# Attention with two expert layers: other weight slots lent to the first eight units, fewer conversions through borrowed slots, single-chunk stores

## The chip, the cores and the metric

The kernel runs on one core of one Trainium2 chip. The metric is the device time of one execution in microseconds (us). Before the change the median of three runs is 1017.11 us (1017.07 to 1017.4). Engines are named as in the profile: PE is the matrix engine, DVE the vector engine, ACT the activation engine, POOL the GpSimd, SP the engine that issues every DMA here.

## The reference

The inputs are q, k, v of shape (4 batches, 8 heads, 576 positions, 64) in float32. Three stages follow each other:

```
q_d, k_d, v_d = means over groups of 4 positions        # 144 positions
out_d  = softmax(q_d k_d^T / 8) v_d, repeated 4 times   # coarse attention
out_l  = softmax over |i - j| < 4 of q k^T / 8, times v # local attention
x  = out_d + out_l                                      # 2304 tokens x 512
y1 = (silu(x Wg) * (x Wv)) Wo                           # 512 -> 1536 -> 512
out = prelu(y1 Win, alpha) Wout                         # 512 -> 2048 -> 512
```

The softmax is written out with its maximum and sum; everything is float32 at the interface.

## The kernel before, in words

**Precision.** A float32 product is made of three passes of a rounded format: each operand is split into a high part and a low part, and hi*hi, hi*lo and lo*hi are summed in PSUM (`mm3`, L472 to L475). The weights arrive as 8-byte elements and are first turned into float32 by bit operations, then split (`w_split`, L124 to L143).

**Weights and slots.** The first layer has 12 slices j of 128 hidden columns, and for each a tile of Wg, Wv and Wo: g0, v0, o0 up to g11, v11, o11. Each tile has a slot of 4 KB in every partition, which takes the raw load (`w_load`, 512 KB, L104 or L106) and then the converted pair. A conversion takes one working buffer (`st_tile`, L116). There are two kinds. The first 3 * NEARLY = 30 conversions sit in one of three weight slots that are not loaded yet (`st_slots`: o10, g11, v11), with two half-buffers each: ACT computes the value (L129) and the top bits (L137), and DVE joins them in one instruction (L139). The later ones sit in a small ring `st` of the pool `hp_` (NST = 2 buffers), where only one buffer is at hand: ACT computes the value (L129), DVE shifts it (L131) and joins the low bits (L132). In both, ACT then rounds to the high part (L142) and POOL subtracts to get the low part (L143). The slots o10, g11, v11 can be loaded only when the first kind has ended: after the slices 0 to 9 the kernel calls `load1` for 10 and 11.

**Attention units.** A unit n is one pair of heads over 288 positions (half of a batch); four units make one block of 288 tokens. There are 32 units and 8 blocks. The first eight units (NPRO = 8) run ahead of the first layer and keep their data in weight slots that are still empty: `pslot` maps qv (q and the windows of v), qs (scores and small buffers), kn (k), vd (v for the means) and bd (the block-diagonal matrix of the local weights), four units each, to the 20 slots from g4 to v10. The units 4 to 7 take qv from the kn slots of the units 0 to 3 and qs from their vd slots, and share `pbd[n % 4]` with them. The later units use a pool of their own with one matrix `bds[0]`. A weight can be loaded into a lent slot only when its unit has let go of it. The phases of a unit are loads (`a_load`, `a_load_v`, `a_load_w`), transposes and means (`a_T`, `a_vd`), scores (`a_QK`), softmax (`a_EXP`, `a_NRM`, whose last step at L419 writes the matrix bd), transposed coarse scores (`a_PT`) and the products with v (`a_PV`, whose matmuls at L450 are the last readers of bd and of the windows).

**Staging of v.** Each local window needs 32 rows of v for 24 positions. `stage(b)` (L257 to L272) copies a batch of v into such windows in memory by DMA, 1.5 MB a batch. Batch 0 is staged first, batch 1 with the loads of unit 8 (`load8`), which wait on SP behind the load of o7 (`gj=7`, `issue_after` at L715), and the batches 2 and 3 wait behind the load of o11 (L777).

**First layer.** For each block and each slice j the kernel runs `m_g`, `m_v` (12 matmuls of 288 columns each) and `m_y` of the slice before (12 matmuls into four PSUM banks Y). ACT's tanh (L512) and DVE's products (L513, L519) make the hidden tile, ACT and POOL split it (L522, L523). Attention units 8 to 31 are threaded between the steps from position 18 on (`at`). In block 0 the conversions of slice j + 1 stand before the steps of slice j. At the end of a block, ACT copies Y to SBUF and SP stores it to y1: two copies of two chunks (128 x 576 values) for the blocks 0 to 6, four copies of one chunk for the last.

**Second layer.** Its 32 weight tiles go through the ring form of conversion while block 7 runs, and then five blocks of up to 512 tokens follow.

**Order.** The program order gives priorities; a planner then writes each engine's queue, by estimated durations, from what is ready and where a slot is free. So an instruction may stand far from its place in the source, and SP's queue above all is ordered by when slots come free in that plan. Once written, each queue is worked through in order.

Of the kernel before, what the change touches and what calls it, by code (L numbers as in the profile page):

```python
# [8 lines left out]
F32 = mybir.dt.float32  # L9
# [7 lines left out]
DRAM = bass.MemoryType.DRAM  # L17


K = dict(kdP=0, qdP=0, dnP=2, ldn=9, lo='asvw0123', NPRO=8, c=5, a1=1, a2=0, OFF=25, oT=3, oE=3, oP=5, oV=11, vd1=2, vd2=1, pre=(1, 1, 0, 0), lo1=0, lo2=1, nst=3, nrm=0, sub=0, nrm1=0, sub1=0, qtA=0, ldw=1, xl1=0, ly=4, l2=3, st2=2, early=1, w2p=1, la=0, bdV=0, sp=9, s2=0, s3=0, gj=7, gs=1, vr=0, kc=0, gD=(0, 0, 0, 0, 0, 0), gP=(0, 2, 8, 8, 0, 0), gA=(0, 0, 0, 0, 0, 0))  # L20


@with_exitstack
def attn_moe_moe2_kernel(
# [13 lines left out]
    nc = tc.nc  # L38
    B, H, S, D = q.shape
    NT, DM = out.shape  # L40
    F1 = w_gate.shape[1] // 128
    F2 = w2_in.shape[1] // 128
    KD = DM // 128
    HB = S // 2
    NB1 = NT // HB
    NP = H // 2
# [8 lines left out]
    SD = S // 4  # L55
    QD = HB // 4
    SW = LW + SD
    NBD, NVD, NVW, NSM, NST = 1, 1, 1, 1, 2
    scale = 1.0 / float(D) ** 0.5
    NEG = -1.0e9 / scale  # L60

# [5 lines left out]
    y1 = dp.tile([DM, NT], F32, name="y1")  # L67
# [3 lines left out]
    Y = [pp.tile([128, 2, 512], F32, name=f"y{i}") for i in range(2)]  # L71
# [7 lines left out]
    hp_ = hstack.enter_context(tc.tile_pool(name="hp", bufs=2))  # L79
# [36 lines left out]
    def st_tile():  # L116
        c = stc[0]
        stc[0] += 1
        if c >= 3 * NEARLY:
            return stp[0].tile([128, 512], F32, tag="st", name="st", bufs=stn[0]), None  # L120
# [27 lines left out]
    pbd = {}  # L148
# [3 lines left out]
    bds = [ap_.tile([128, 2, NW, 128], F32, name=f"bd{i}", bufs=1) for i in range(NBD)]  # L152

    def coords(n):
        blk, hp = divmod(n, NP)
        b, half = divmod(blk, 2)
        return b, half, hp, blk

    order = [f"{kind}{j}" for j in range(F1 - 8, F1) for kind in "gvo"]
    st_slots = order[5 * NP:][:K["nst"]]  # L160
    NEARLY = F1 - 2
    pslot = {(what, n): order[4 * i + n] for i, what in enumerate(("qv", "qs", "kn", "vd", "bd")) for n in range(NP)}
    for n in range(NP):
        pslot["qv", n + NP] = pslot["kn", n]
        pslot["qs", n + NP] = pslot["qs" if K["vr"] else "vd", n]
    NPRO = K["NPRO"]
    srs = [ap_.tile([128, 8], F32, name=f"sr{i}", bufs=1) for i in range(4)]

    def at_(n, shape, tag):
        return wp.tile(shape, F32, tag=pslot[tag, n], name=tag)  # L170
# [66 lines left out]
    def a_load_w(n):  # L237

        b, half, hp, blk = coords(n)
        if n < NP:  # L240
            pbd[n] = at_(n, [128, 2, NW, 128], "bd")
            (nc.vector if K["bdV"] else nc.gpsimd).memset(pbd[n], 0.0)
        if n >= NPRO:
            hu[n]["vw"] = ap_.tile([128, NW, 2, D], F32, tag="vw", name="vw", bufs=NVW)
        t = hu[n]["vw"]
        for h in range(2):
            w0 = ((b * H + 2 * hp + h) * 2 + half) * NW * 128
            nc.sync.dma_start(out=t[:, :, h], in_=vwin[w0:w0 + NW * 128, :].rearrange("(w p) c -> p w c", p=128))
# [27 lines left out]
    def a_T(n, A):  # L276
# [24 lines left out]
        else:  # L301
            for r in range(NW):
                nc.tensor.transpose(A[:, 0, QB * r:QB * (r + 1)], d["qn"][:, r].rearrange("p h c -> p (h c)"), idn)
            if K["qtA"]:
                nc.scalar.copy(out=qT[:, 0:HB], in_=A[:, 0, 0:HB])
            else:
                nc.vector.tensor_copy(qT[:, 0:HB], A[:, 0, 0:HB])
        if half == 0:
            if n < NPRO and K["kdP"]:
                kq = kT[:, 3:S + 3].rearrange("c (g r) -> c g r", r=4)  # L310
# [81 lines left out]
    def a_NRM(n):  # L392
        d = hu[n]
        sm, loc, sr = d["sm"], d["loc"], d["sr"]
        s4 = sr[:, 0:6].rearrange("p (h w) -> p h w", h=2)
        if not d["la"]:
            nc.vector.tensor_reduce(out=s4, in_=loc, axis=AX.X, op=ALU.add)
        if not d["act"]:
            nc.vector.reduce_sum(sr[:72, 6:8], sm[:72, :, LW:SW], axis=AX.X)
        nc.vector.tensor_scalar_add(out=sr, in0=sr, scalar1=1e-9)  # L400
        nc.vector.reciprocal(out=sr, in_=sr)
        nrm = K["nrm1" if n < NPRO else "nrm"]
        if nrm == 2:
            for h in range(2):
                for w in range(NW):
                    nc.scalar.mul(out=loc[:, h, w], in_=loc[:, h, w], mul=sr[:, NW * h + w:NW * h + w + 1])
        else:
            (nc.vector if nrm else nc.gpsimd).tensor_tensor(out=loc, in0=loc, in1=s4.unsqueeze(3).to_broadcast([128, 2, NW, SWIN]), op=ALU.mult)
        dn = n < 2 * NP and K["dnP"]
        if dn == 2:  # L410
            for h in range(2):
                nc.scalar.mul(out=sm[:72, h, LW:SW], in_=sm[:72, h, LW:SW], mul=sr[:72, 6 + h:7 + h])
        else:
            (nc.gpsimd if dn else nc.vector).tensor_tensor(out=sm[:72, :, LW:SW], in0=sm[:72, :, LW:SW],
                                in1=sr[:72, 6:8].unsqueeze(2).to_broadcast([72, 2, SD]), op=ALU.mult)
        d["bd"] = pbd[n % NP] if n < NPRO else bds[n % NBD]
        for i in range(NS):
            ps = slice(SWIN * i, SWIN * (i + 1))
            nc.vector.transpose(out=d["bd"][ps, :, :, SWIN * i:SWIN * (i + 1)], in_=loc[ps])  # L419
# [52 lines left out]
    def mm3(o, lhi, llo, rhi, rlo, first, last):  # L472
        nc.tensor.matmul(o, lhi, rhi, start=first, stop=False)  # L473
        nc.tensor.matmul(o, lhi, rlo, start=False, stop=False)  # L474
        nc.tensor.matmul(o, llo, rhi, start=False, stop=last)  # L475
# [6 lines left out]
    def load1(j):  # L482
        for kind in "gvo":
            w_load(kind, j, f"{kind}{j}")
# [41 lines left out]
    def m_y(blk, j):  # L526
        ph, pl = hid.pop((blk, j))
        o = W[f"o{j}"]
        for e in range(KD):
            es = slice(e * 128, (e + 1) * 128)  # L530
            mm3(Y[e // 2][:, e % 2, :HB], o[:, 0, es], o[:, 1, es], ph, pl, j == 0, j == F1 - 1)
        if j == F1 - 1:
            for e in range(KD):
                if blk == NB1 - 1:
                    ys = side2.tile([128, 512], F32, tag="sy", name="sy", bufs=2)[:, :HB]
                elif e % 2:
                    continue
                else:
                    ys = hp_.tile([128, 2, HB], F32, tag="st", name="ys", bufs=NST)
                n = 1 if blk == NB1 - 1 else 2  # L540
                src = Y[e // 2][:, e % 2, :HB] if n == 1 else Y[e // 2][:, :, :HB]
                nc.scalar.copy(out=ys, in_=src)  # L542
                nc.sync.dma_start(
                    out=y1[e * 128:(e + n) * 128, blk * HB:(blk + 1) * HB].rearrange("(e p) t -> p e t", p=128),
                    in_=ys.unsqueeze(1) if n == 1 else ys)


    blocks2 = [512, 512, 512, 512, 256]
# [81 lines left out]
    if True:  # L630
        make_identity(nc, ident)
        for tok in K["lo"]:
            if tok == "s":
                stage(0)
            elif tok in "avw":
                for n in range(NP):
                    {"a": a_load, "v": a_load_v, "w": a_load_w}[tok](n)
            elif tok == "x":
                for n in range(NP):
                    a_load_v(n)  # L640
                    a_load_w(n)
            else:
                load1(int(tok))
# [21 lines left out]
        def a_all(n, A):  # L665
            a_T(n, A)
            if K["vd1"] == 0:
                a_vd(n)
            a_QK(n, A)
            gate(n, 0)  # L670
            if K["vd1"] == 1:
                a_vd(n)
            a_EXP(n)
            a_NRM(n)
            gate(n, 1)
            if K["vd1"] == 2:
                a_vd(n)
            a_PT(n, A)
            if K["vd1"] == 3:
                a_vd(n)  # L680
            a_PV(n, A)
# [16 lines left out]
        for n in range(NP, NPRO):  # L698
            a_load(n)
            a_load_w(n)  # L700
# [5 lines left out]
        def load8():  # L706
            if B > 1:
                stage(1)
            a_load(NPRO)
            a_load_v(NPRO)  # L710
            a_load_w(NPRO)
# [27 lines left out]
        OFF = K["OFF"]  # L739
        at(0 if NPRO == NP else OFF - 7, lambda: a_pre(NPRO))  # L740
        for n in range(NPRO, NHU):
            if n < 2 * NP:
                c = K["c"]
                p, oT, oE, oP, oV = c * (n - NP) + 1, 1, 1, c - 1, c
            else:
                p, oT, oE, oP, oV = OFF + K["sp"] * (n - 2 * NP), K["oT"], K["oE"], K["oP"], K["oV"]
# [12 lines left out]
        for i, (blk, j) in enumerate(fts):  # L759
            if blk == NB1 - 1 and j == 0:  # L760
                assert not ev, ev.keys()
                astack.close()
                side2 = ctx.enter_context(tc.tile_pool(name="p2a", bufs=1, side="right"))
# [5 lines left out]
            if blk == 0:  # L769
                while pc[0] <= min(j + K["early"], F1 - 1):  # L770
                    prep1(pc[0])
                    pc[0] += 1
                    if pc[0] == NEARLY:
                        load1(F1 - 2)
# [9 lines left out]
            if i > 0:  # L784
                m_y(*fts[i - 1])
# [14 lines left out]
        for t in range(len(f2s)):  # L800
            if True:
                i, j = f2s[t]
# [8 lines left out]
            if SK <= t < len(f2s):  # L811
                i, j = f2s[t - SK]
# [32 lines left out]
```

## Time and profile before

| what | us |
|---|---|
| median of three runs | 1017.11 |
| the profiled execution | 1017.97 |
| its span | 1015.9 |
| PE busy | 969.7 (95%) |
| DVE busy | 478.9 (47%) |
| ACT busy | 306.8 (30%) |
| POOL busy | 383.5 (38%) |

The page divides the span into 40 slices of 25.4 us and shows the busy share of each in tenths:

```profile
PE   5489789999999999999999999999999999999998
...
DVE  5577864555444555444532769622222322322232
ACT  3869632222221322222323556312111101211111
POOL 5868763234322344222223435624223322322222
PEclk9999899999999999999999999999999999999999
DMA  8998741132111321110103883102000100100010
```

A digit 9 is 90% or more. PE is below 9 only in the first six slices and in the last; PEclk below 9 means that the clock granted to PE was lower in part of that slice. The rows in the section below come from the views of the trace: stretches (busy time of each engine between two times), waits (who waited for whom, in total), timelines (instructions in order of time), the chain of waits (what released each step of the chain that ended last), and groups of instructions.

### The profile page before, as it was taken

The numbers are of one execution on the slowest core, as the hardware profiler recorded it, in microseconds if no ns is written. First come the engines' busy times: TensorE is split into PE (matmuls) and PEld (weight loads), VectorE is DVE, ScalarE is ACT, GpSimd is POOL, SyncE is SP. The second block draws the span as 40 slices with busy tenths as digits, with TensorE's granted clock in tenths as the row PEclk, the third lists the DMA queues.
The fourth block names the chain that finished last, engine by engine and source line by source line (L and its number), as shares of the span: only waits on it lengthen the run. The fifth ranks groups of instructions, "written<-read, shape, count | busy, mean of one in ns | idle before, by whom it ended". The sixth has DMA issues, their size and how long they took to land.

```text
span 1015.9 us, 19233 instructions
## 1 busy us (share of the span) xinstructions
PE 969.7 (95%) x7760; PEld 865.3 (85%) x7760; DVE 478.9 (47%) x1015; ACT 306.8 (30%) x690; POOL 383.5 (38%) x492
## 2 busy tenths in 40 slices
PE   5489789999999999999999999999999999999998
PEld 4379679999999999999999998888888888888897
DVE  5577864555444555444532769622222322322232
ACT  3869632222221322222323556312111101211111
POOL 5868763234322344222223435624223322322222
PEclk9999899999999999999999999999999999999999
DMA  8998741132111321110103883102000100100010
GB/s 202 290 315 283 184 93 27 35 73 59 38 46 21 76 50 41 40 26 18 43 9 116 282 254 122 42 1 63 22 0 21 52 1 1 42 11 1 0 43 22
DMA packets 135894, 77.81 MB, mean 77 GB/s; under 512 B 97406, under 2 KB 127102, under 8 KB 135038
## 3 DMA queue, kind: packets, MB, share of 16 engines
q1 hardware_dynamic: 135804, 76.58, 27.0%
q8 instruction: 60, 0.98, 0.4%
q14 instruction: 30, 0.25, 0.1%
HBM read 67.12 MB, written 15.73 MB: 82 GB/s over the span
## 4 chain that ended last, share of the span: by engine, by line
PE 82%; SPq 4%; DVE 4%; DMA 3%; POOL 3%; issue 2%; ACT 2%; POOLq 0%; DVEq 0%; ACTq 0%
PE y L610 7%; PE y L612 6%; PE y L611 6%; PE g L473 6%; PE v L474 6%; PE v L473 6%; PE v L475 6%; PE g L474 6%; PE g L475 6%; PE y L473 4%; PE y L475 4%; PE y L474 4%; PE h L473 3%; PE h L475 3%; PE h L474 3%
## 5 line engine op out<-in xcount | busy, mean ns | idle before, releaser
L598 POOL TENSOR_TENSOR gl<-t,gh 128x512 fp32r<-128x512 f32 (+1 forms) x80 | 97.0, 1214 | 250.9 <-ACT gh L597 244.4
L597 ACT CAST gh<-t 128x512 fp32r<-128x512 f32 (+1 forms) x80 | 46.2, 578 | 278.7 <-DVE t L594 239.2
L473 PE MATMUL g<-xh,w 128*128 128x288 f32 x384 | 117.4, 306 | 10.0 <-DVE u L513 4.4
L475 PE MATMUL g<-xh,w 128*128 128x288 f32 x384 | 115.1, 300 | 1.9 <-POOL w L143 1.8
L473 PE MATMUL v<-xh,w 128*128 128x288 f32 x384 | 116.0, 302 | 0.6 <-ACT w L142 0.4
L474 PE MATMUL v<-xl,w 128*128 128x288 f32 x384 | 115.3, 300 | 0.0
L474 PE MATMUL g<-xl,w 128*128 128x288 f32 x384 | 115.0, 300 | 0.0
L474 PE MATMUL y<-pl,w 128*128 128x288 f32 x384 | 113.8, 298 | 1.3 <-POOL pl L523 1.2
L475 PE MATMUL v<-xh,w 128*128 128x288 f32 x384 | 113.8, 296 | 0.6 <-POOL w L143 0.6
L610 PE MATMUL y<-w,gh 128*128 128x512 f32 x288 | 113.2, 393 | 1.0 <-ACT sy L542 1.0
L475 PE MATMUL y<-ph,w 128*128 128x288 f32 x384 | 113.0, 296 | 0.0
L611 PE MATMUL y<-w,gh 128*128 128x512 f32 x288 | 112.8, 392 | 0.0
L612 PE MATMUL y<-w,gl 128*128 128x512 f32 x288 | 112.0, 392 | 0.0
L513 DVE SCALAR_TENSOR_TENSOR u<-u,g 128x288 f32<-128x288 f32 x96 | 43.3, 451 | 144.1 <-ACT u L512 144.1
L473 PE MATMUL y<-ph,w 128*128 128x288 f32 x384 | 111.0, 301 | 0.2 <-ACT ph L522 0.2
L523 POOL TENSOR_TENSOR pl<-u,ph 128x288 fp32r<-128x288 f32 x96 | 79.8, 832 | 59.4 <-ACT ph L522 58.6
L143 POOL TENSOR_TENSOR w<-st,w 128x512 fp32r<-128x512 f32 x52 | 70.2, 1356 | 60.7 <-ACT w L142 60.5
L473 PEld LDWEIGHTS g<-xh,w 128*128 128x128 f32 x384 | 73.5, 191 | 12.9 <-DVE u L513 5.7
L592 DVE TENSOR_SCALAR t<-h,alpha 128x512 f32<-128x512 f32 (+1 forms) x40 | 27.9, 697 | 110.7 <-PE h L475 109.5
L512 ACT ACTIVATE u<-g 128x288 f32<-128x288 f32 x96 | 39.4, 410 | 122.8 <-PE g L475 121.3
L475 PEld LDWEIGHTS g<-xh,w 128*128 128x128 f32 x384 | 73.7, 192 | 2.7 <-POOL w L143 2.4
L473 PEld LDWEIGHTS v<-xh,w 128*128 128x128 f32 x384 | 72.8, 190 | 2.3 <-DVE u L519 1.0
(190 smaller groups left out, 2143.4 us busy)
## 6 DMA issues: line engine op xcount, KB each, us to landing
raw<-in_moe_w_out_dram SPq DMA_DIRECT2D x28, 512.0 KB
raw<-in_moe_w_in_dram SPq DMA_DIRECT2D x16, 512.0 KB
raw<-in_moe_w_gate_dram SPq DMA_DIRECT2D x12, 512.0 KB
raw<-in_moe_w_val_dram SPq DMA_DIRECT2D x12, 512.0 KB
vw<-vwin SPq DMA_DIRECT2D x48, 96.0 KB
out_dram<-os SPq DMA_DIRECT2D x18, 256.0 KB
sy<-y SPq DMA_DIRECT2D x16, 256.0 KB
y<-ys SPq DMA_DIRECT2D x14, 288.0 KB
```

The source lines that it names most:

```text
L143: eng.tensor_sub(w[:, 1], st, f32(w[:, 0]))
L473: nc.tensor.matmul(o, lhi, rhi, start=first, stop=False)
L474: nc.tensor.matmul(o, lhi, rlo, start=False, stop=False)
L475: nc.tensor.matmul(o, llo, rhi, start=False, stop=last)
L512: nc.scalar.activation(out=u, in_=GV[0][:, :HB], func=AF.Tanh, scale=0.5)
L513: nc.vector.scalar_tensor_tensor(out=u, in0=u, scalar=1.0, in1=GV[0][:, :HB], op0=ALU.add, op1=ALU.mult)
L523: nc.gpsimd.tensor_sub(pl, u, f32(ph))
L597: nc.scalar.copy(out=gh[:, :n], in_=t[:, :n])
L598: nc.gpsimd.tensor_sub(gl[:, :n], t[:, :n], f32(gh[:, :n]))
L610: nc.tensor.matmul(o, gh[:, ms], ohi, start=(j == 0), stop=False)
L611: nc.tensor.matmul(o, gh[:, ms], olo, start=False, stop=False)
L612: nc.tensor.matmul(o, gl[:, ms], ohi, start=False, stop=(j == F2 - 1))
```

## The change

The data of the first eight units changes places: bd goes to o6, g7, v7, o7, and kn (with qv of the units 4 to 7) to v9, o9, g10, v10. A fifth matrix `pbd[4]` takes the slot o11; it is cleared with the others' loads, one more POOL memset. The units 0 to 3 use `pbd[0..3]`, the units 4 and 6 `pbd[4]`, and the units 5 and 7 the matrix `bds[0]` of the later units. NEARLY goes from 10 to 8 slices, so that 24 conversions sit in the slots o10, g11, v11 and the slices 8 and 9 join 10 and 11 in the ring; the call of `load1` for 10 and 11 comes after slice 7. The ring gets three buffers of 512 values instead of two of 576. The loads of unit 8 with the staging of batch 1 wait behind o9 instead of o7. The blocks 0 to 6 store y1 in four copies of one chunk.

```diff
-K = dict(..., gj=7, ...)
+K = dict(..., gj=9, ...)
...
-    NBD, NVD, NVW, NSM, NST = 1, 1, 1, 1, 2
+    NBD, NVD, NVW, NSM, NST = 1, 1, 1, 1, 3
...
-    st_slots = order[5 * NP:][:K["nst"]]
-    NEARLY = F1 - 2
-    pslot = {(what, n): order[4 * i + n] for i, what in enumerate(("qv", "qs", "kn", "vd", "bd")) for n in range(NP)}
+    st_slots = order[5 * NP:][:3]
+    NEARLY = F1 - 4
+    pslot = {(what, n): order[4 * i + n] for i, what in enumerate(("qv", "qs", "bd", "vd", "kn")) for n in range(NP)}
+    pslot["bd", NP] = order[5 * NP + 3]
...
-        if n < NP:
+        if n <= NP:
             pbd[n] = at_(n, [128, 2, NW, 128], "bd")
-            (nc.vector if K["bdV"] else nc.gpsimd).memset(pbd[n], 0.0)
+            nc.gpsimd.memset(pbd[n], 0.0)
...
-        d["bd"] = pbd[n % NP] if n < NPRO else bds[n % NBD]
+        d["bd"] = pbd[n] if n < NP else pbd[NP] if n < NPRO and n % 2 == 0 else bds[0]
...
             for e in range(KD):
-                if blk == NB1 - 1:
-                    ys = side2.tile([128, 512], F32, tag="sy", name="sy", bufs=2)[:, :HB]
-                elif e % 2:
-                    continue
-                else:
-                    ys = hp_.tile([128, 2, HB], F32, tag="st", name="ys", bufs=NST)
...
+                pool, tag, n = (side2, "sy", 2) if blk == NB1 - 1 else (hp_, "st", NST)
+                ys = pool.tile([128, 512], F32, tag=tag, name="ys", bufs=n)[:, :HB]
+                nc.scalar.copy(out=ys, in_=Y[e // 2][:, e % 2, :HB])
+                nc.sync.dma_start(out=y1[e * 128:(e + 1) * 128, blk * HB:(blk + 1) * HB], in_=ys)
```

## Rows read from the trace of the kernel before

**Rows 1.** Page, part 1: busy time and share of the span.

```profile
PE 969.7 (95%) x7760; PEld 865.3 (85%) x7760; DVE 478.9 (47%) x1015; ACT 306.8 (30%) x690; POOL 383.5 (38%) x492
```

**Rows 2.** Stretches: length, PE, PEld, DVE, ACT, POOL busy, PEclk, DMA share, GB/s.

```profile
53.00:68.00 15.00, 10.64 (x207) 8.77 (x207) 13.11 (x38) 10.84 (x33) 11.02 (x18) 0.96 0.97 317
...
56.00:108.00 52.00, 47.60 (x540) 43.88 (x534) 40.03 (x89) 41.99 (x104) 38.76 (x45) 0.97 0.88 298
108.00:143.00 35.00, 27.74 (x279) 23.84 (x278) 34.22 (x62) 17.64 (x36) 25.96 (x30) 0.90 0.65 149
149.00:555.00 406.00, 406.00 (x4251) 387.02 (x4250) 193.59 (x511) 104.72 (x274) 128.44 (x215) 1.00 0.19 44
...
60.00:80.00 20.00, 17.44 (x191) 15.81 (x191) 15.45 (x46) 15.21 (x46) 9.75 (x15) 0.91 1.05 369
...
116.00:124.00 8.00, 3.99 (x17) 3.19 (x16) 7.96 (x15) 3.38 (x8) 6.80 (x7) 0.62 0.70 169
```

**Rows 3.** Waits of PE from 100 to 152 us: total, times, longest.

```profile
PE g L473 <- ACT w L142: 2.2, 1, 2.2
PE g L473 <- DVE u L513: 2.0, 2, 1.1
PE g L475 <- POOL w L143: 1.8, 1, 1.8
PE v L475 <- POOL w L143: 0.6, 1, 0.6
```

**Rows 4.** Timeline of PE: start, duration, instruction; two stretches of one projection each.

```profile
73.18 0.29 PE L475 MATMUL g<-xh,w 128*128 128x288 f32 x1
...
74.38 0.29 PE L475 MATMUL g<-xh,w 128*128 128x288 f32 x1
...
121.56 0.44 PE L473 MATMUL g<-xh,w 128*128 128x288 f32 x1
...
123.48 0.44 PE L475 MATMUL g<-xh,w 128*128 128x288 f32 x1
```

**Rows 5.** Timeline of SP's issues between 54 and 96 us.

```profile
54.73 0.50 SPq L104 DMA_DIRECT2D raw<-in_moe_w_out_dram  x1
...
83.30 12.37 SPq L104 DMA_DIRECT2D raw<-in_moe_w_out_dram  x2
95.73 0.53 SPq L257 DMA_DIRECT2D vwin<-in_v_dram  x1
```

**Rows 6.** Waits of SP's queue from 53 to 96 us.

```profile
SPq L104 <- PE att L450: 9.8, 1, 9.8
SPq L106 <- DMA vwin<-in_v_dram: 7.5, 2, 4.5
```

**Rows 7.** Groups by form, 50 to 150 us: busy, mean ns, idle before.

```profile
L139 DVE SCALAR_TENSOR_TENSOR st<-st 128x512 int32<-128x512 int32 x22 | 20.4, 934 | 8.7 <-ACT st L137 7.2 <-POOL xl L460 0.8 <-POOL pl L523 0.7
...
L137 ACT ACTIVATE st<-raw 128x512 int32<-128x512 uint8 x21 | 14.0, 665 | 0.0
...
L131 DVE TENSOR_SCALAR st<-st 128x512 int32<-128x512 int32 x6 | 5.9, 995 | 0.0
```

**Rows 8.** Timeline of DVE and POOL around the longest shift.

```profile
112.30 2.63 DVE L131 TENSOR_SCALAR st<-st 128x512 int32<-128x512 int32 x1
...
112.54 1.30 POOL L143 TENSOR_TENSOR w<-st,w 128x512 fp32r<-128x512 f32 x1
```

**Rows 9.** Chain of waits, from issue of a load to its landing.

```profile
109.53 2.62 DMA kn<-in_k_dram
```

**Rows 10.** Instructions of line 542: ns min/median/max, first and last start.

```profile
L542 ACT COPY ys<-y x14: 627/640/641, 148.4 to 554.8; 128x576 f32<-128x576 f32 x14
...
L542 ACT COPY sy<-y x4: 387/395/404, 623.8 to 627.7; 128x288 f32<-128x288 f32 x4
```

**Rows 11.** Timeline around the matrices bd of the units 6 and 4.

```profile
70.47 1.51 DVE L419 STREAM_TRANSPOSE bd<-qs 32x192 f32<-32x192 f32 x4
...
71.73 0.67 PE L450 MATMUL att<-bd,qv 128*64 128x96 f32 x12
```

More of the change, by code (lines that the diff above doesn't have):

```diff
@@ L17 @@
 DRAM = bass.MemoryType.DRAM
-K = dict(kdP=0, qdP=0, dnP=2, ldn=9, lo='asvw0123', NPRO=8, c=5, a1=1, a2=0, OFF=25, oT=3, oE=3, oP=5, oV=11, vd1=2, vd2=1, pre=(1, 1, 0, 0), lo1=0, lo2=1, nst=3, nrm=0, sub=0, nrm1=0, sub1=0, qtA=0, ldw=1, xl1=0, ly=4, l2=3, st2=2, early=1, w2p=1, la=0, bdV=0, sp=9, s2=0, s3=0, gj=7, gs=1, vr=0, kc=0, gD=(0, 0, 0, 0, 0, 0), gP=(0, 2, 8, 8, 0, 0), gA=(0, 0, 0, 0, 0, 0))
+K = dict(kdP=0, qdP=0, dnP=2, ldn=9, lo='asvw0123', NPRO=8, c=5, a1=1, a2=0, OFF=25, oT=3, oE=3, oP=5, oV=11, vd1=2, vd2=1, pre=(1, 1, 0, 0), lo1=0, lo2=1, nst=3, nrm=0, sub=0, nrm1=0, sub1=0, qtA=0, ldw=1, xl1=0, ly=4, l2=3, st2=2, early=1, w2p=1, la=0, bdV=0, sp=9, s2=0, s3=0, gj=9, gs=1, vr=0, kc=0, gD=(0, 0, 0, 0, 0, 0), gP=(0, 2, 8, 8, 0, 0), gA=(0, 0, 0, 0, 0, 0))
 @with_exitstack
@@ L533, in m_y @@
             for e in range(KD):
-                if blk == NB1 - 1:
-                    ys = side2.tile([128, 512], F32, tag="sy", name="sy", bufs=2)[:, :HB]
-                elif e % 2:
-                    continue
-                else:
-                    ys = hp_.tile([128, 2, HB], F32, tag="st", name="ys", bufs=NST)
[L540 to L545, printed above, removed]
+                pool, tag, n = (side2, "sy", 2) if blk == NB1 - 1 else (hp_, "st", NST)
+                ys = pool.tile([128, 512], F32, tag=tag, name="ys", bufs=n)[:, :HB]
+                nc.scalar.copy(out=ys, in_=Y[e // 2][:, e % 2, :HB])
+                nc.sync.dma_start(out=y1[e * 128:(e + 1) * 128, blk * HB:(blk + 1) * HB], in_=ys)
     blocks2 = [512, 512, 512, 512, 256]
```

## The prediction

> **What bounds the kernel now.** I read the page first: PE is busy for 95% of the span [rows 1], so the question is where the rest lies. Then the stretches: from 149 to 555 us PE is busy for 406.00 of 406.00 us [rows 2], so every later block follows block 0 rigidly, and a microsecond won or lost before 149 us is one at the end. Nothing that only moves DVE, ACT or POOL work inside that long stretch can show. What is left is block 0 with the units 4 to 7 beside it. There PE is short of 52.00 us by 4.4 between 56 and 108, and of 35.00 us by 7.3 between 108 and 143 [rows 2]. The waits of PE say what ended last in the second stretch: a projection waited 2.2 us for ACT's rounding of a weight, its third pass 1.8 us for POOL's low part, a later one 0.6 us for the same, and 2.0 us went to DVE's product that frees the PSUM bank [rows 3]. The reader is to see that 4.6 us of these are late weights.
>
> Late weights mean late conversions, and two things make them late. First, loads: SP waits 9.8 us for the last product of unit 7 before it can load the second of two Wo tiles (the row from 83.30 lasts 12.37 us because of that), and 7.5 us for the stagings of the batches 2 and 3, which went out right behind the free slot o11 at 54.73 us [rows 5, 6]. Second, between 60 and 80 us POOL is busy for 9.75 of 20 us and DVE for 15.45 [rows 2]: conversions could run there, but the DMA engines are full (share 1.05) with 369 GB/s, a good part of it stagings. From 108 to 143 us DVE is then busy for 34.22 of 35.00 us.
>
> **The change part by part.**
>
> *Slots of bd and kn.* The four slots o6, g7, v7, o7 come free after the units 0 to 3 and not after 4 to 7. With g4 to v6, that makes twelve weight tiles (slices 4 to 7) that no late unit holds. What remains behind the units 4 to 7 are slices 8 and 9, g10 and v10. o11 is now lent until unit 6 has ended, so its load, and behind it both stagings, leave SP after about 76 us instead of at 54.73. That takes 2 x 1.5 MB out of the full stretch: at 369 GB/s [rows 2], 8 us of DMA time and the 7.5 us of SP waits [rows 6].
>
> *What this gives the conversions.* In 60 to 80 us POOL has 20 - 9.75 = 10.25 us free and DVE 20 - 15.45 = 4.55 us. At 0.934 us of DVE each [rows 7], about 5 conversions move forward. By then POOL's part of a conversion is over 1.3 us [rows 8], so the ones that PE waits for come 5 x 1.3 = 6.5 us sooner or more, beyond the 2.2 + 1.8 us by which PE stood still. I take the late weights out in full: **-4.6 us** [rows 3].
>
> *The clock.* In 116 to 124 us the granted clock was 0.62 of full on average, behind the pause of PE [rows 2]. The matmuls of that projection follow each other at (123.48 - 121.56) / 8 = 0.240 us, against (74.38 - 73.18) / 9 = 0.133 us in one at full speed [rows 4]: the lower and the upper level of 1.2 and 2.4 GHz, nearly. Twelve matmuls at 0.107 us more are 1.3 us, and without the pause they go: **-1.3 us**. The lower end is 0, if a pause stays.
>
> *Slices 8 and 9 in the ring.* Six conversions lose ACT's top bits (6 x 0.665 = 4.0 us of ACT) and gain a shift on DVE. A shift took 0.995 us on average, 6.0 for six [rows 7], and at the worst 2.63, beside POOL's subtraction of 1.30 [rows 8], 15.8 for six. They fall about where DVE is full or just before. Between 56 and 108 us DVE has 52 - 40.03 = 12.0 us free [rows 2]; six shifts and five joins that came forward are 6.0 + 4.7 = 10.7. It fits on paper, and I don't trust the fit: a quarter of the 6.0 us is charged, **+1.5 us**. Ends: -2.0, if ACT's relief also ends the waits for the product [rows 3], and +6.0, the mean row; 15.8 is a tail.
>
> *NEARLY at 8.* o10, g11 and v11 are free six conversions sooner, so the slices 10 and 11 are loaded sooner: the 0.6 us is in the sum already. Three ring buffers let a third conversion run ahead; no gain is booked.
>
> *Loads of unit 8 behind o9.* o9's slot hangs on unit 5, o7's hung on unit 7, so the 95.73 of [rows 5] can become about 80 us. Unit 8 belongs to block 2 and is not urgent: 0. If SP's queue keeps a load that needs unit 7 ahead of it, it stays at 95.73, also 0. Queued behind this load on SP are the staging of batch 1 and k, q and v of unit 8, for which DVE's transposes and POOL's sums would wait in their own queues.
>
> *bd sharing.* Unit 6's transposes at 70.47 must now wait for unit 4's products, 71.73 + 0.67 [rows 11]: 1.9 us on DVE, with products of the first layer and PE's projection at 73 to 74 us [rows 4] as cover. Its price without cover is 1.9 us; I take 0, because a unit of block 1 is needed only after block 0. Units 7 and 8 come long after their matrix is free. The added memset depends on nothing, so the planner can put it into any idle time of POOL: 0, and at most about one instruction of POOL, 1.30 [rows 8], if it can't.
>
> *Stores of y1.* Four copies of 0.395 replace two of 0.640 [rows 10]: 1.58 against 1.28 us, 0.3 us of ACT in each of seven blocks. With three buffers the fourth copy waits for the first store to land; by the nearest row, 2.62 us [rows 9] less two copies, ACT is held for some 1.8 us. PE meanwhile has 24 matmuls of 0.133 us, 3.2 us, before it needs a freed bank. PE is full in that stretch [rows 2], so 0; without cover it is 7 x 1.8 = 12.6 us, which I leave to the tail.
>
> **Sum.** -4.6 - 1.3 + 1.5 = -4.4 us. The profiled execution took 1017.97 us (2.1 us around its span of 1015.9), which becomes 1013.6; it lay 0.86 us above the median of the runs, so the forecast is 1017.11 - 4.4 = **1012.7 us**, with 1008.5 to 1015 as its own range. About 0.2%, 2.0 us, is what a measurement can tell from no change.
>
> **Rivals.**
>
> *A. The shift is the bound (slower).* From 108 us on DVE has 0.78 us free in 35 [rows 2]. If the shifts of slices 8 and 9 still fall there, DVE is later by 6.0 us [rows 7], PE's banks are freed later by as much, and the weights come no sooner, since they pass through DVE too: 1017.1 + 6.0 = 1023.1. It decides from the point where more than one shift lies behind 108 us. For it: the 2.63 us of [rows 8], and DVE's fullness. Against it: the 12.0 us that DVE has before. The Trainium skill (SBUF — State Buffer, section "Who interferes with whom") speaks for it: a vector instruction with one tensor and a scalar in the fast mode, and a GpSimd instruction, take one pair of ports, and the one that starts first keeps it for its whole length. The trace agrees in that a shift became longer by about the length of POOL's work.
>
> *B. More than forecast.* PE also lacks 15 - 10.64 = 4.4 us between 53 and 68 us [rows 2], where attention, not weights, is late; a new order could close it, together with the 2.0 us of the product: 1017.1 - 4.6 - 1.3 - 2.0 - 4.4 = 1004.8. Against it: DVE is busy for 13.11 of these 15 us.
>
> *C. DVE's fullness turns the gain into a new wait.* PE comes sooner and waits for DVE's products in 108 to 143 us instead of for weights: 1017.1 within 2 us. For it: the 34.22 of 35.00 us. Against it: work leaves that stretch.
>
> *D. The loads don't move.* The planner may keep SP's order, with a load for unit 7's slots ahead of the others: the gain is gone, the 1.5 us stay: 1018.6.
>
> **How the numbers follow.** Forecast 0.45, A 0.22, B 0.13, C 0.13, D 0.07. Faster by over 0.2%: nearly all of the forecast, B, and a few hundredths of C: 0.60. Within 0.2%: most of C and half of D: 0.12. Slower: A, the rest of D and C: 0.28. The range goes from B's value, 1005, to 1022, which takes in all cases but A's upper half and the tails.
>
> **What would show it.** Right: the stagings of batches 2 and 3 issued after 76 us; the SP waits for unit 7 and for stagings gone before 76; POOL busy for over 13 us in 60 to 80; no PE wait for a weight over 0.5 us after 104; no fall of the clock after 100; the first store of y1 about 4 us sooner than now, and PE full from there on. Wrong: a group of twelve shifts before 150 us with a mean over 1.0 us and PE waiting for DVE's products (A or C), ACT idle for stores behind the copies at block ends with PE waiting, or the same SP wait for unit 7 ahead of weights of slices 6 and 7 (D).

## The result and the profile after

The changed kernel is slower: 1029.49 us (1027.30 to 1031.26, four runs) against 1017.09, a ratio of 1.0120 [1.0099, 1.0142]. 1012.7 was forecast, and the time lies outside the range. The profiled execution has a span of 1026.7 us, 10.8 more than before.

The page, part 1, and the same stretches as in [rows 1, 2] (length, PE, PEld, DVE, ACT, POOL busy, PEclk, DMA share, GB/s), kernel after:

```profile
PE 974.8 (95%) x7760; PEld 870.3 (85%) x7760; DVE 485.1 (47%) x1021; ACT 304.0 (30%) x698; POOL 386.0 (38%) x493
```

```profile
53.00:68.00 15.00, 13.18 (x234) 11.85 (x232) 14.34 (x43) 11.88 (x37) 11.63 (x19) 1.00 1.00 302
56.00:108.00 52.00, 43.32 (x504) 39.82 (x497) 40.90 (x88) 37.52 (x96) 38.43 (x45) 0.93 0.96 307
108.00:143.00 35.00, 27.43 (x268) 24.13 (x266) 29.44 (x56) 14.38 (x30) 19.89 (x23) 0.85 0.57 137
149.00:555.00 406.00, 406.00 (x4231) 386.90 (x4231) 195.47 (x512) 104.92 (x284) 128.40 (x216) 1.00 0.18 41
...
60.00:80.00 20.00, 17.59 (x174) 16.40 (x173) 16.10 (x44) 18.17 (x52) 12.85 (x14) 1.00 1.00 342
```

PE is full again from 149 us on, so the time was lost in block 0, as the prediction's first paragraph says it must be. From 53 to 68 us the kernel after is ahead (PE 13.18 against 10.64 us). From 56 to 108 us it has 4.3 us less of PE, and in both later stretches a lower clock. The clock as such got no better: 0.85 against 0.90 from 108 to 143 us.

The place is read best from the tanh behind each gate projection, which marks how far PE is. Slices 3, 4, 8, 9 and 11 of block 0 on ACT (start, duration, instruction, idle before); first before, then after:

```profile
74.77 0.41 ACT L512 ACTIVATE u<-g 128x288 f32<-128x288 f32 x1 [0.74 <-PE g L475]
...
85.38 0.40 ACT L512 ACTIVATE u<-g 128x288 f32<-128x288 f32 x1
...
110.52 0.40 ACT L512 ACTIVATE u<-g 128x288 f32<-128x288 f32 x1
...
123.95 0.41 ACT L512 ACTIVATE u<-g 128x288 f32<-128x288 f32 x1 [4.01 <-PE g L475]
...
135.37 0.41 ACT L512 ACTIVATE u<-g 128x288 f32<-128x288 f32 x1 [0.72 <-PE g L475]
```

```profile
70.71 0.41 ACT L513 ACTIVATE u<-g 128x288 f32<-128x288 f32 x1 [0.63 <-PE g L476]
...
88.79 0.41 ACT L513 ACTIVATE u<-g 128x288 f32<-128x288 f32 x1
...
114.27 0.41 ACT L513 ACTIVATE u<-g 128x288 f32<-128x288 f32 x1 [1.38 <-POOL w L143]
...
131.36 0.40 ACT L513 ACTIVATE u<-g 128x288 f32<-128x288 f32 x1
...
150.98 0.40 ACT L513 ACTIVATE u<-g 128x288 f32<-128x288 f32 x1
```

At slice 3 the change is 4.1 us ahead, at slice 4 it is 3.4 behind, at slice 8 3.8, at slice 9 7.4, at slice 11 15.6 (some work of block 1 comes sooner in return: at its slice 5 the lag is 10.6 us). So there are two losses, one between the slices 3 and 4 and one from slice 9 on. Waits of PE after, 68 to 104 us and 104 to 160 us:

```profile
PE y L475 <- POOL pl L524: 3.2, 1, 3.2
PE g L474 <- DVE u L514: 2.5, 2, 1.9
...
PE g L474 <- DVE u L514: 2.9, 1, 2.9
PE g L474 <- ACT w L142: 1.6, 1, 1.6
```

**First loss.** Two things meet in this stretch. One is the matrix that unit 6 shares with unit 4. DVE's transposes of unit 6 and PE's products of the units 4 and 6, kernel after (compare [rows 11]):

```profile
72.61 0.67 PE L451 MATMUL att<-bd,qv 128*64 128x96 f32 x12
...
73.39 1.51 DVE L420 STREAM_TRANSPOSE bd<-qs 32x192 f32<-32x192 f32 x4
...
76.93 0.72 PE L451 MATMUL y<-bd,qv 128*64 128x96 f32 x12
```

The transposes begin when unit 4's products end, 2.9 us later than in [rows 11]. The other is that weights arrive early, and their conversions do nearly what was predicted (POOL 12.85 us in 60 to 80 against 9.75; over 13 was predicted): eight of them stand on ACT between the tanh of slice 3 and that of slice 4, where before there were four. Slice 4's projection ends at 76.1 us, its tanh runs at 88.79. Which of the two costs how much, this trace alone does not say.

**Second loss.** SP's queue, waits from 53 to 76 us, then the issue of the last weight (the Wg of slice 9, g9), kernel after:

```profile
SPq L106 <- PE att L451: 7.1, 1, 7.1
...
110.24 0.64 SPq L106 DMA_DIRECT2D raw<-in_moe_w_gate_dram  x1
```

Up to 76 us SP's waits for unit 7 and for stagings were to be gone, and they are; but there is a new one, 7.1 us for unit 4's products, since that unit's memory now lies in v9. g9's own load left at 106.35 us before and leaves 3.9 us later. Shifts, joins behind them, and joins without a shift on DVE, 50 to 160 us, after (compare [rows 7]):

```profile
L132 DVE SCALAR_TENSOR_TENSOR st<-raw,st 128x512 int32<-128x512 int32 x12 | 15.2, 1269 | 0.1
...
L139 DVE SCALAR_TENSOR_TENSOR st<-st 128x512 int32<-128x512 int32 x16 | 15.1, 942 | 4.4 <-ACT st L137 4.4
...
L131 DVE TENSOR_SCALAR st<-st 128x512 int32<-128x512 int32 x12 | 9.4, 780 | 0.0
```

Twelve ring conversions instead of six cost DVE a shift and a slow join each, and nine of them, g9's first, start at 121.92 us or later. In the chain of waits from 121 to 151 us such shifts and joins take 5.7 and 5.6 us; in the kernel before there is none of either in it. From the tanh of slice 9 to that of slice 11 it takes 19.6 us, before 11.4.

### The profile page after: what moved, and what is told of

The parts are those of the page before. It is cut to its first block, busy times and chain, and to the rows that moved or that the text cites. A ratio compares the mean times of both kernels' runs of the same rounds, so it can differ in the third digit from the quotient of the medians.

```text
span 1026.7 us, 19274 instructions
## 1 busy us (share of the span) xinstructions
PE 974.8 (95%) x7760; PEld 870.3 (85%) x7760; DVE 485.1 (47%) x1021; ACT 304.0 (30%) x698; POOL 386.0 (38%) x493
## 4 chain that ended last, share of the span: by engine, by line
PE 84%; DVE 6%; DMA 3%; ACT 3%; SPq 2%; issue 1%; POOL 1%; DVEq 0%; ACTq 0%; POOLq 0%
PE y L603 6%; PE g L474 6%; PE y L605 6%; PE y L604 6%; PE v L475 6%; PE v L474 6%; PE g L476 6%; PE g L475 6%; PE v L476 6%; PE y L474 5%; PE y L476 4%; PE y L475 4%; PE h L474 3%; PE h L476 3%; PE h L475 3%
## 5 line engine op out<-in xcount | busy, mean ns | idle before, releaser
L474 PE MATMUL y<-ph,w 128*128 128x288 f32 x384 | 112.8, 305 | 3.9 <-ACT ph L523 2.2
L476 PE MATMUL y<-ph,w 128*128 128x288 f32 x384 | 113.7, 298 | 0.0
L524 POOL TENSOR_TENSOR pl<-u,ph 128x288 fp32r<-128x288 f32 x96 | 80.0, 833 | 74.1 <-ACT ph L523 73.9
L474 PEld LDWEIGHTS g<-xh,w 128*128 128x128 f32 x384 | 74.3, 194 | 16.3 <-DVE qs L456 5.3
L474 PEld LDWEIGHTS y<-ph,w 128*128 128x128 f32 x384 | 71.4, 190 | 9.3 <-issue 4.2
L475 PEld LDWEIGHTS y<-pl,w 128*128 128x128 f32 x384 | 72.9, 190 | 4.7 <-POOL pl L524 4.3
```

Of the source, the lines that this page charges most:

```text
L524: nc.gpsimd.tensor_sub(pl, u, f32(ph))
```

## The experiments

Each kernel is one of the two with a few lines edited. Differences below are those of the ratios, in us of 1017 (after: 12.2); by the 95% intervals, one between two edited kernels is uncertain by 2 to 3 us. All times, with the tanh of the slices 4, 9 and 11 of block 0 (us in the profiled execution):

```
run           time us  ratio to before           tanh 4   9     11
before        1017.1                              85.4  124.0  135.4
after         1029.5   1.0120 [1.0099, 1.0142]    88.8  131.4  151.0
b_slots       1024.5   1.0078 [1.0063, 1.0094]    87.3  128.2  143.1
b_ring        1018.3   1.0016 [1.0007, 1.0025]    84.5  116.3  137.6
b_store       1017.4   1.0006 [0.9995, 1.0017]    84.3  120.7  134.3
b_gj          1021.1   1.0042 [1.0027, 1.0057]    83.9  126.0  139.1
a_u6          1027.7   1.0102 [1.0082, 1.0121]    87.6  130.2  153.5
a_vog         1023.9   1.0063 [1.0040, 1.0085]    88.5  131.1  143.8
a_stage       1029.9   1.0123 [1.0105, 1.0140]    88.9  129.7  151.2
b_stage       1025.9   1.0083 [1.0057, 1.0110]    90.9  123.6  145.6
bs_h15        1026.6   1.0098 [1.0079, 1.0118]    88.8  123.8  148.2
a_h15         1024.4   1.0077 [1.0057, 1.0097]    86.4  128.1  143.9
av_h15        1024.9   1.0086 [1.0065, 1.0107]    85.6  132.0  143.6
av_u6h15      1023.7   1.0082 [1.0054, 1.0111]    86.5  130.8  143.6
a_pair        1025.3   1.0083 [1.0068, 1.0098]    89.1  124.6  147.6
a_u6v         1027.7   1.0100 [1.0085, 1.0115]    87.4  130.2  146.4
a_pair_u6     1019.4   1.0025 [1.0013, 1.0037]    86.5  116.7  139.6
a_pair_u6n    1016.3   0.9997 [0.9983, 1.0012]    88.3  118.8  136.2
a_pair_u567n  1023.9   1.0069 [1.0054, 1.0083]    89.5  117.1  144.2
b_pair        1013.6   0.9970 [0.9957, 0.9984]    84.3  115.6  131.6
```

The table can be read as a whole: the time nearly follows the last column. Runs with slice 11 at 131 to 140 us take 1014 to 1021, those at 143 to 153 take 1024 to 1030. The column of slice 4 does not sort them: the run with 88.3 takes 1016.3, that with 85.6 takes 1024.9. So what is won or lost up to slice 4 does not decide the time; what is lost by slice 11 nearly does.

### Parts of the change alone

**b_slots**: the kernel before with the new places.

```diff
-enumerate(("qv", "qs", "kn", "vd", "bd"))
+enumerate(("qv", "qs", "bd", "vd", "kn"))
+    pslot["bd", NP] = order[5 * NP + 3]
...
-        if n < NP:
+        if n <= NP:
...
-        d["bd"] = pbd[n % NP] if n < NPRO else bds[n % NBD]
+        d["bd"] = pbd[n] if n < NP else pbd[NP] if n < NPRO and n % 2 == 0 else bds[0]
```

> The kernel before, with only the new places of the first units' data (bd in o6 to o7, kn in v9 to v10, the fifth matrix in o11, units 4 to 7 on two matrices); ring, stores and the place of unit 8's loads stay as before. Theory S (the new places and the shared matrices hold up unit 6 and the PSUM banks, and lead to the queue order that makes slice 9 late): 8 to 14 us slower than before, with unit 6's products after 76 us and PE waiting over 5 us between 68 and 104 us. Theory R (the shifts of the ring form on a full DVE): within 3 us of before or faster. Theory L (loads of unit 8 and stagings ahead of weights): 3 to 6 us slower, since the stagings of batches 2 and 3 move but unit 8's loads don't.

**b_ring**: only the slices 8 and 9 in the ring; **b_store**: only the single copies and three ring buffers; **b_gj**: only the wait of unit 8's loads.

```diff
-    NEARLY = F1 - 2
+    NEARLY = F1 - 4
```

> The kernel before, with only 24 conversions in borrowed slots (slices 8 and 9 through the ring, two buffers). Theory R: 5 us or more slower, with shifts of about 1 us each between 104 and 140 us. Theories S and L: within 3 us of before.

```diff
-    NBD, NVD, NVW, NSM, NST = 1, 1, 1, 1, 2
+    NBD, NVD, NVW, NSM, NST = 1, 1, 1, 1, 3
...
+                ys = pool.tile([128, 512], F32, tag=tag, name="ys", bufs=n)[:, :HB]
```

> The kernel before, with only the four single copies per block into three ring buffers. All theories: within 2 us of before; PE waits for nothing from 149 to 555 us. If stores hold ACT and with it PE, 2 us or more slower, about 0.3 to 2 us in each of seven blocks.

```diff
-K = dict(..., gj=7, ...)
+K = dict(..., gj=9, ...)
```

> The kernel before, with only the loads of unit 8 behind o9 instead of o7. Theory L: 3 us or more slower, since the staging of batch 1 and k, q, v of unit 8 now stand ahead of o7 and slices 8 and 9 on the queue of DMAs. Theories S and R: within 2 us of before.

That is +7.9 us for the places, +1.6 for the ring, +4.3 for unit 8's wait, and nothing that can be measured for the stores: 13.8 where together they cost 12.2, which agrees within the uncertainty. The places are the largest. So S came out at its lower edge and L as written, R did not (5 us or more were expected for the ring), and the stores do nothing, as expected. In b_gj the staging of batch 1 leaves at 78.66 us, ahead of five tiles of the slices 7 and 8, and unit 8's loads of k stand ahead of two of them, o8 and o7; o7 leaves only at 98.21, and PE waits 2.3 us for the conversion of each.

b_ring holds more than its total. PE's waits there, 100 to 152 us (tiles carry a letter, a to l for the slices 0 to 11):

```profile
PE g L473 <- ACT wgl L142: 3.4, 1, 3.4
PE g L473 <- ACT wgk L142: 2.9, 1, 2.9
```

Slice 9's tanh comes at 116.3 us, 7.7 sooner than before, and PE no longer waits for g9. But it waits for the Wg of the slices 10 and 11 instead, and slice 11 is 2.2 us later than before. So an early slice 9 alone brings nothing here.

### The stagings: the forecast's main step by itself

**b_stage** (before) and **a_stage** (after) let the stagings of the batches 2 and 3 go only behind the load of v10.

```diff
-                            with tc.issue_after(wdma[f"o{F1 - 1}"]):
+                            with tc.issue_after(wdma["v10"]):
```

> The kernel before, with only the stagings of the batches 2 and 3 moved: behind the load of v10 instead of behind that of o11. This is the step of the prediction that was to bring the gain, by itself. P (as predicted: the stagings at 55 us delay weight loads, and with them gone the conversions come forward and PE no longer waits for weights after 104 us): 1011 to 1014.5 us, the waits for POOL's and ACT's weight parts of 4.6 us nearly gone. N (weights wait for units and for DVE, not for transfers): 1016 to 1018 us. If P holds, the prediction failed in what else the change brings, not in this.

> The kernel after, with the stagings of the batches 2 and 3 let go only behind the load of v10 instead of behind that of o11. T (the stagings, which went out at 87.84 us, fill the transfers just when the last weights are to come): g9's load, issued at 110.24 us, goes out at 104 to 106, slice 9's tanh comes at 125 to 128 us instead of 131.4, and the time is 1024 to 1027 us. U (g9's place is given back only when unit 7 has ended, at 103.5 us, and the stagings had room): within 2 us of 1029.5.

b_stage took +8.4 us where a gain was predicted, and fits neither expectation. The conversions did come forward: POOL is busy for 12.18 us from 60 to 80 instead of 9.75. But slice 4 is 5.5 us late, slice 9 has its tanh at 123.61, where it was, and slice 11 is 10.2 us late. What happened behind slice 9, SP's queue shows. The loads of o10 and v11, first before, then b_stage, and two pieces of b_stage's chain of waits:

```profile
121.13 0.35 SPq L104 DMA_DIRECT2D raw<-in_moe_w_out_dram  x1
...
122.92 0.41 SPq L106 DMA_DIRECT2D raw<-in_moe_w_val_dram  x1
```

```profile
119.38 7.97 SPq L206 DMA_DIRECT2D kn<-in_k_dram  x4
...
129.97 0.51 SPq L272 DMA_DIRECT2D vwin<-in_v_dram  x1
130.58 0.53 SPq L104 DMA_DIRECT2D rawok<-in_moe_w_out_dram  x1
131.21 0.39 SPq L106 DMA_DIRECT2D rawvl<-in_moe_w_val_dram  x1
```

```profile
110.96 10.66 DMA vwin<-in_v_dram
...
130.58 4.83 DMA rawok<-in_moe_w_out_dram
```

The stagings now stand among the last loads, together with unit loads, and those leave 9.5 and 8.3 us later; PE waits 4.7 us for o10's conversion. At 55 us the stagings had delayed weights whose earlier arrival, as b_stage shows, moves no tanh from slice 2 on forward by more than 0.4 us.

In a_stage the loads of o10, g11, v11 and v10 leave ahead of the stagings, and g9 at 106.31 instead of 110.24, as early as in the kernel before. The tanh of slice 9 gains 1.7 us, that of slice 11 nothing (U): the place of the stagings is not what makes the kernel after slow. Nor is it the moment of g9's load alone. ACT in a_stage:

```profile
119.75 0.40 ACT L430 COPY pt<-att 72x288 f32<-72x288 f32 x1 [1.96 <-PE att L427]
120.05 0.68 ACT L129 ACTIVATE st<-rawgj 128x512 f32<-128x512 f32 x1
```

g9's conversion waits for no load here; it stands behind the copy that follows a later attention unit's softmax, as it does in the kernel after, at 121.92 us. So its place in ACT's queue holds it, and an earlier load does not change that.

### Are early conversions in the way?

The hold: conversions from slice 5 on wait for unit 7's scores.

```diff
-gD=(0, 0, 0, 0, 0, 0), gP=(0, 2, 8, 8, 0, 0), gA=(0, 0, 0, 0, 0, 0)
+gD=(0, 0, 0, 0, 0, 15), gP=(0, 2, 8, 8, 0, 15), gA=(0, 0, 0, 0, 0, 15)
```

> The kernel of the run before with only the stagings moved (1025.9 us), with the conversions from slice 5 on held until unit 7's scores are on ACT's and DVE's queues. There seven conversions stood between the tanh of slice 3 and that of slice 4 in ACT's queue, against four in the kernel before; held, three do. Q (conversions that come early cost time, since they stand in ACT's queue ahead of a tanh whose projection is done): slice 4's tanh at 83 to 86 us instead of 90.9, PE idle between 68 and 104 us under 1.5 us instead of 4.2, 1014 to 1019 us. X (the loss is that the stagings now meet the last loads and unit 8, behind 104 us, where a product waited 4.7 us for slice 10's Wo): slice 4 may come sooner, but 1023 to 1027 us stay.

> The kernel after, with the same hold: conversions from slice 5 on behind unit 7's scores; three conversions instead of eight between the tanh of slice 3 and that of slice 4. Q: slice 4's tanh at 82 to 85 us instead of 88.8, PE idle between 68 and 104 us 2 to 4 us instead of 6.9, and unit 7 ends sooner, so that g9 comes sooner: 1020 to 1025 us; the losses behind the late g9 stay in part. S (unit 6 waiting for unit 4's matrix sets slice 4, whatever the conversions do): slice 4's tanh stays at 87 to 89 and the time at 1027 to 1031.

In bs_h15 Q missed: slice 4 came 2.1 us sooner, the time stayed (X). In a_h15 slice 4 came 2.4 us sooner and the whole 4.4 us, as Q said; but slice 6, level with the kernel after (102.0 against 101.6 us), had lost it again, so the gain is not slice 4's. From slice 3 to 4 it now takes 14.8 us (71.6 to 86.4), against 18.1 after and 10.6 before: the conversions in ACT's queue explain less than half of the first loss.

### The late g9

**a_vog** converts slice 9 in the order v, o, g.

```diff
-        for kind in "gvo":
+        for kind in ("vog" if j == 9 else "gvo"):
```

> The kernel after, with the conversions of slice 9 written in the order v, o, g instead of g, v, o. O (the ring of three conversion buffers is served strictly in the order of the program, so g9, the last weight to arrive, holds v9 and o9, which lie loaded since 74 us): v9's and o9's conversions move from behind 122 us to before 115, PE has slice 9's value projection to do while g9 comes, and 3 to 6 us go: 1023.5 to 1026.5 us. G (g9 itself is late, and what stands behind it costs nothing, since the gate projection comes first in any order): 1028.5 to 1030.5 us.

It took 5.8 us off (O). g9 still leaves at 110.31 us and slice 9 keeps its tanh at 131.05, but slice 11 has it at 143.8 instead of 151.0. The ring hands out its buffers in the order of the program, and in the kernel after g9 held v9 and o9, whose loads had left by 74.1 us, out of it.

**av_h15** has both, **av_u6h15** also unit 3's matrix for unit 6, **a_u6** that matrix alone, **a_u6v** the matrix and v, o, g.

> The kernel after, with both: the hold on the conversions from slice 5 on, and slice 9 converted in the order v, o, g (which gave 5.6 us by itself). Q: the two causes are at different places and add up: 1015 to 1019.5 us, level with the kernel before. If the hold only pushes work into the full stretch behind 104 us: 1021 to 1026.

> As the run with hold and v, o, g, and unit 6 with unit 3's matrix instead of unit 4's. Q with the shared matrix as a third, small part: 1 to 3 us below the run without it, 1012.5 to 1018 us. If sharing costs nothing once the conversions are held: the same within 1.5 us, or longer by o7, which is then lent until unit 6 has ended.

```diff
-pbd[NP] if n < NPRO and n % 2 == 0 else bds[0]
+pbd[NP] if n == NP else pbd[3] if n == 6 else bds[0]
```

> The kernel after, with one edit: unit 6 takes the matrix of unit 3 (slot o7) instead of sharing the fifth one with unit 4. S (the shared matrix is the cause of the first loss, the 7 us between the slices 3 and 4): unit 6's transposes no longer wait for unit 4's products, its PSUM bank is free about 4 us sooner, the tanh of slice 4 comes at 84 to 86 us instead of 88.8, and the whole takes 1024 to 1026.5 us. U (early conversions crowd the late units on DVE and ACT, sharing or not): slice 4 stays at 87 to 89 us and the time at 1028.5 to 1030.5. In both the later losses at the slices 9 to 11 stay, 10 us or more, since g9 still waits for unit 7.

> The kernel after, with the two edits that were tried singly: unit 6 with unit 3's matrix (1027.7 by itself) and slice 9 converted as v, o, g (1023.9 by itself). If they are two causes at two places: the tanh of the slices 4 to 8 as in the run with unit 3's matrix (87.6 to 109.3 us), those of 10 and 11 as in the run with v, o, g or sooner (137, 143), and 1019 to 1022 us. If slice 9's weights set the end whatever comes before: 1023 to 1025.

None of these sums came out. Hold and v, o, g together give what v, o, g gives alone. With unit 3's matrix most of the first loss goes by slice 8: PE from 68 to 104 us, a_u6 (after had 29.14 at 0.91, before 35.97):

```profile
68.00:104.00 36.00, 33.44 (x341) 31.80 (x340) 26.16 (x52) 28.51 (x65) 26.09 (x25) 0.95 0.88 269
```

and slice 8 is at 109.35 us instead of 114.27. At slice 4 only 1.2 us of it are to be seen (S expected 3 to 5), and five conversions stand between the tanh of the slices 3 and 4 on ACT, not eight: the edit moved them too. Yet slice 9 stands at 130.2, since g9 leaves at 115.90 us, later than in any other run read here, and ACT sits idle 5.4 us until it lands. What was won ahead of slice 9 is lost in front of it; in a_u6v g9 leaves at 115.4. These runs point to g9's place, which unit 7 holds.

**a_pair** takes it from there: pairs of slots for the units 4 to 7.

```diff
+    for n in range(NP):
+        pslot["vd", n], pslot["kn", n] = order[3 * NP + 2 * n], order[3 * NP + 2 * n + 1]
```

> The kernel after, with the memory of the units 4 to 7 dealt out in pairs: unit 4 in g8, v8, unit 5 in o8, g9, unit 6 in v9, o9, unit 7 in g10, v10 (after has unit 7 in g9 and v10). G (the late g9, released by unit 7, starts the ring 10 to 20 us late): g9's load goes out before 80 us instead of at 110.24, slice 9's tanh at 118 to 123 us instead of 131.4, the time 1018 to 1023 us. D (DVE's shifts and joins beside units 9 and 10 are the limit, whenever g9 comes): slice 9 sooner, but slice 11's tanh still at 147 or later and the time 1026 to 1030.

> As the run with pairs, and unit 6 with unit 3's matrix. If sharing is a cost of its own (it lifted PE's idle time between 68 and 104 us from 2.6 to 6.9 us): 2 to 5 us below the run with pairs alone, 1014 to 1019 us. If it is hidden anyway by the wait for later weights: within 1.5 us of that run.

> Pairs, unit 3's matrix for unit 6, and only the slices 10 and 11 in the ring (as before the change). If six shifts on DVE cost what the run with the ring alone showed (2.0 us): 2 us below the run with pairs and unit 3's matrix, 1012 to 1017 us, and level with the kernel before or better. If not: the same as that run within 1 us.

The load of g9 in a_pair:

```profile
74.37 0.37 SPq L106 DMA_DIRECT2D rawgj<-in_moe_w_gate_dram  x1
```

Slice 9 comes 6.8 us sooner and 3.8 us are gone, less than G said; slice 11 is still at 147.6, as D said, and PE waits for the weights of the slices 10 and 11. But now the matrix counts: a_pair_u6 is 5.9 us faster than a_pair, where a_u6 was within the uncertainty of the kernel after. And the two slices taken out of the ring again give another 2.8 us. Together that is 12.5 us: level with the kernel before, though unit 8's loads still wait behind o9, which cost 4.3 us in b_gj.

**a_pair_u567n** gives the units 5, 6 and 7 the matrices of the units 1 to 3; **b_pair** deals out pairs in the kernel before.

```diff
-pbd[NP] if n == NP else pbd[3] if n == 6 else bds[0]
+pbd[NP] if n == NP else pbd[n - 4] if n < NPRO else bds[0]
```

> The run with pairs, unit 3's matrix for unit 6 and two slices in the ring (1016.3 us), and besides the units 5 and 7 with the matrices of the units 1 and 3 and unit 6 with unit 2's, so that no late unit waits for another's matrix. If sharing costs wherever it stands: unit 7 ends sooner and 1 to 4 us go, 1012 to 1015.5 us. If only unit 6 was late by it: within 1.5 us of 1016.3, or longer, since v7 and v6's neighbours are then lent longer and load behind unit 7.

```diff
+    for n in range(NP):
+        pslot["vd", n], pslot["bd", n] = order[3 * NP + 2 * n], order[3 * NP + 2 * n + 1]
```

> The kernel before, with one edit: its rows of vd and bd are dealt out in pairs, so that unit 7 leaves g9 and holds g10 and v10 (and o7, as before). If g9 is late for unit 7's sake there as well (its projection of slice 9 waited 2.2 us for ACT's and 1.8 us for POOL's part of a weight): those 4.0 us go at most, 1012.5 to 1015.5 us. If slice 9 is bound by DVE there: 1016 to 1019 us.

The first is 7.3 us slower than a_pair_u6n: o7 is lent until unit 7 ends, and PE waits 1.8 us for its conversion. So whatever sharing costs the units 5 and 7, it is less here than lending o7, g7 and v7 for longer. The second beats both kernels, 1013.56 us, a ratio of 0.9970 [0.9957, 0.9984] to the kernel before. Its load of g9, the tanh of the slices 9 and 11, and PE's longest waits from 104 to 160 us:

```profile
74.90 2.08 SPq L106 DMA_DIRECT2D rawgj<-in_moe_w_gate_dram  x1
```

```profile
115.59 0.40 ACT L514 ACTIVATE u<-g 128x288 f32<-128x288 f32 x1
...
131.60 0.41 ACT L514 ACTIVATE u<-g 128x288 f32<-128x288 f32 x1
```

```profile
PE g L475 <- DVE u L515: 1.9, 2, 1.0
PE y L476 <- POOL pl L525: 1.8, 3, 0.8
PE g L477 <- POOL wgj L143: 0.9, 1, 0.9
```

The 4.0 us for the weight of slice 9 in [rows 3] are down to 0.9, and the kernel is 3.0 us faster (1.6 to 4.4). This is most of the gain that the prediction wanted, had by dealing eight slots out in another way, so that g9 falls to unit 5.

## Why the prediction was wrong, step by step

**Where the bound was put: right.** Block 0 sets the time: from 165 to 555 us PE is busy for at least 389.9 of 390 us in every run.

**"I take the late weights out in full": the step that failed.** The waits of [rows 3] were real: b_pair, where 3.1 of the 4.0 us for g9 go, is 3.0 us faster. But 4.0 of the 4.6 us belong to one weight. Both long waits lie in one projection of the kernel before, the one that ends in slice 9's tanh at 123.95, and so wait for g9:

```profile
118.47 0.61 PE L473 MATMUL g<-xh,w 128*128 128x288 f32 x1 [2.18 <-ACT w L142]
...
121.15 0.61 PE L475 MATMUL g<-xh,w 128*128 128x288 f32 x1 [1.83 <-POOL w L143]
```

The prediction did not ask which weight it was, and let five conversions moved forward anywhere make this one sooner. The change frees tiles of the slices 6 and 7, and leaves g9 with unit 7, which it makes later. The text even listed "slices 8 and 9, g10 and v10" as what remains behind the late units, and gave it no price. Early conversions of other weights came (POOL 12.85 us in 60 to 80), and slice 9 came 7.4 us later all the same, with PE still waiting 3.2 us for weights from 104 to 160 us (5.0 before). And g9 was only the first in a row: with slice 9 early, as in b_ring and a_pair, the slices 10 and 11 were late.

**The stagings: right in time, wrong in sign.** They left at 87.84 us, after 76 as predicted. Counting the DMA time taken out of the full stretch as gain left out where it goes. Moved alone they cost 8.4 us; the trace shows them among the last loads, and no run separates this from the 4.1 us of PE that b_stage has lost by 104 us.

**bd sharing at 0: wrong.** The wait was there and its length was right within a us: transposes 2.9 us later, 1.9 predicted. The cover was not: the price is 5.9 us when slice 9 does not hide it (a_pair to a_pair_u6), and 1.8, not to be told from nothing, when it does (after to a_u6). How it comes about is open. Unit 6's products come 1.3 us later on PE than before (76.93 against 75.65), but in a_u6 they come at 77.74, later still, and PE has 4.3 us more from 68 to 104 us all the same.

**Ring at +1.5: the size came out, by luck.** +1.6 alone, +2.8 in the runs with pairs. But the +1.6 of b_ring is the rest of two larger effects, slice 9 7.7 us sooner and 9.9 us more from slice 9 to slice 11, and not a quarter of six shifts. The 12 shifts of the kernel after took 0.78 us on average, below the 0.995 of [rows 7]; the joins behind them, which the sum left out, took 1.27 against 0.94 without a shift. What was not predicted either is the ring's order, worth 5.8 us in a_vog. Rival A gave the right direction and nearly the half of the loss. Shifts and joins do hold the chain of waits behind g9, but taking the two slices out of the ring gave back no more than 2.8 us; in the kernel after as it stands that was not tried. The longest shift after, and POOL beside it:

```profile
138.47 2.56 DVE L131 TENSOR_SCALAR st<-st 128x512 int32<-128x512 int32 x1
...
138.73 1.27 POOL L143 TENSOR_TENSOR w<-st,w 128x512 fp32r<-128x512 f32 x1
```

The Trainium skill (SBUF — State Buffer, section "Who interferes with whom") says that a vector instruction in its two-port mode and a GpSimd instruction share ports, and that the one waits for the other; the trace agrees, with 2.56 us beside POOL's work where other shifts took 0.41.

**Unit 8's loads at 0: wrong.** +4.3 us alone: they and the staging of batch 1 stand on SP ahead of weights of the slices 7 and 8. Within the whole change it wasn't tried by itself.

**Stores at 0: right.** 1.0006 [0.9995, 1.0017]. ACT waited 1.1 us for stores in the whole execution.

**The clock at -1.3: wrong.** The granted clock from 108 to 143 us was 0.85 of full on average, 0.90 before; PE paused there still, now 2.9 us for DVE's product and 1.6 us for a weight.

**What stays open.** How sharing costs its 5.9 us, and why the hold gives 4.4 us in the kernel after and nothing beside v, o, g; the order that is computed for all queues changes with every edit, and no run separates that from the edit's own effect. The sums above are therefore sizes of edits in this kernel, not constants.

## What to carry to other kernels

When a trace shows waits for weights, name the weight, then its slot, then the last user of the slot, and ask whether the change moves that one, and which weight PE would wait for next; here many other weights came early, and the kernel was 12.2 us slower. A transfer that is taken out of a full stretch has to be looked for where it lands, above all ahead of the last loads of the same queue. A wait priced at "hidden" can be hidden by the very wait that one means to remove, so it is priced again without that.
